# Sparse attention and a PReLU layer on one core: a third value block cast head by head, and the first 600 pieces of a hand-listed order rearranged

## The chip, the cores and the metric

The kernel runs on one core of a Trainium2 chip. A core has a matrix engine (TensorE, "PE" in the profile), whose weight loads are listed apart ("PEld"); a vector engine (VectorE, "DVE"); a scalar engine (ScalarE, "ACT"); a general one (GpSimd, "POOL"); and SyncE ("SP"), which here only issues transfers. Sixteen DMA engines move the data of every queue. Each engine runs its own instructions strictly in its own order, and waits by semaphores for the others. The metric is the device time in microseconds (us) of one execution, and lower is better.

## The reference, cut to what matters

There are 4 batches and 8 heads, each with 768 positions of 64 numbers. Heads 0, 2 and 6 ("retrieval") attend to all earlier positions. The other five ("streaming") attend to the last 64 positions and to the first 4.

```
scores = q @ k^T / 8, masked
a = exp(scores) / sum(exp(scores))
x = a @ v                        # heads side by side: 3072 tokens x 512
h = x @ w_in                     # 512 -> 2048
g = max(h, 0) + alpha * min(h, 0)
out = g @ w_out                  # 2048 -> 512
```

## The kernel before, in words

The heads are taken in pairs, (2,6), (1,5), (0,4) and (3,7), and the work of one batch and one pair is a segment n = 0..15 (n = 4 * batch + pair, L99). Segments 0 to 3 are batch 0. The tokens go through the second layer in eight blocks t: 512 and 256 of each batch (L592).

The program is cut into 1071 named pieces. `ORDER` (L14 to L71) lists their names, written out, and the loop at the end (L826) emits them in just this order. Every engine's queue, and SP's queue of loads, follows from this list: a piece stands on its engine behind all pieces of that engine that are listed earlier. PSUM, where PE writes, has 8 banks. A piece takes banks when it is listed (L145), the one free for longest among those it may use, and has to wait until the piece that gave the bank back has really run. The names are:

- `Lq n`, `Lk n`, `Lv n`: loads of q, k, v of a segment, issued on SP (L204, L216, L231); fp32, 0.393 MB for a pair, a little more for streaming values, whose last 24 rows come as a transfer of their own (L249).
- `Cq n`, `Ck n.head`: their casts to bf16. For segments 0 to 3 nearly all are on POOL (L301, L302). `Cv n`: the cast of both heads' values (L351), on POOL for n < 6. `Cv n.head` casts one head alone (L346): head 0 of the pair on POOL, head 1 on VectorE. A streaming head then has its first four rows copied into six more places (L311).
- `Tq n`, `Tk n`: six transposes on PE each (L360), and `tq n`, `tk n.head`: the copies out of PSUM (L370, L378).
- `S n.head.m`: a part of the scores (L448, L489); `s n.head.m`: its exp, on ACT; `m n.head.m`: a mask on VectorE, from segment 4 on. From segment 4 on, scores that are listed close together are collected (L420): if both heads have at least 576 columns in the collection, the matmuls of the two heads, which use 64 rows of the array each, are interleaved (L433 in the profile), otherwise they are issued one after the other (L426).
- `A n.head`: the product with the values (L559). `a n.head`: division on VectorE (L569, L570). `X n`, `x n`: transposition into `xT` (L584, L589), one part per pair.
- `P t.f`, `p t.f`, `g t.f`: the first layer on PE (L604), the negative part on ACT (L609), the PReLU sum on VectorE (L616). `P0.f.0`, `.1`, `.2` for f < 6 are parts of the first block, which need the pairs 0 and 1, then 2, then 3 (L810). `O t.s.u`, `o t.s`: the second layer (L624) and its way out (L630, L634).
- `wi x`, `wo x`: the weights, issued on POOL (L712, L716), 0.26 MB each as written for `wi`.
- Fills: `kz3` (a zeroed K buffer, POOL), `ro` (the tail of both score buffers of retrieval heads, VectorE, L735), `nz`, `kfz` (POOL), `id` (the identity matrix, POOL), `warm0` to `warm2` (45 matmuls without use at the start, L704).

In `before` only the values of segment 3 are cast head by head:

```
772        if n == 3:
773            for hh in range(2):
774                item(f"Cv{n}.{hh}", cast_v_head, n, hh)
```

Of the kernel before, what the change touches and what calls it, by code (L numbers as in the profile page):

```python
# [23 lines left out]
g1.0 P1.6 P1.4 Lq8 p1.2 one Lq7 g1.2 nz1 wo1 nz0 Tq4 P0.6 wo0 P0.5.0 tk5.1 g0.0 P0.5.1 Lk7 P0.4.0 P0.4.1 p0.6 P0.4.2
g0.6 P0.5.2 p1.6 P0.14 g1.6 Cq6 Tq6 Ck6.0 p1.4 p0.14 g1.4 tq6 P0.13 p0.4 P0.10 g0.14 g0.4 p0.5 kfz0 P1.8 wo2 P0.9 Lv5
p0.13 tq4 g0.5 p1.8 g0.13 g1.8 p0.9 P0.11 Lv4 g0.9 p0.10 S4.0.4 S5.1.2 S4.1.3 Lv6 S4.0.0 p0.11 P1.10 s4.0.0 P0.8 P0.7
g0.10 g0.11 p1.10 S5.0.0 Lk9 g1.10 s5.1.2 p0.8 s4.0.4 g0.8 S4.1.1 S5.0.2 p0.7 S4.1.2 P0.12 s4.1.2 wo3 O0.1.0 s5.0.2
g0.7 s4.1.3 O0.1.1 Ck6.1 p0.12 S5.1.0 g0.12 m4.0.0 s4.1.1 S5.1.1 S4.0.3 m5.1.2 S5.0.1 Lq9 s5.0.0 S4.0.5 S4.1.4 Cv5 Cq7
s4.1.4 Lk8 m4.1.4 m5.0.0 Cq8 s5.0.1 P0.15 O0.3.0 s5.1.1 p0.15 s5.1.0 Tk6 Ck7.0 P1.14 g0.15 S4.1.5 s4.0.3 S4.0.1 s4.0.5
S4.1.0 S4.0.2 O0.3.1 O0.1.2 m5.1.1 m5.1.0 m4.0.4 s4.0.2 p1.14 m5.0.1 s4.1.0 Ck7.1 tk6.1 m4.1.3 m4.1.0 m5.0.2 O0.3.2  # L30
O0.0.0 tk6.0 Tk7 m4.1.1 A5.0 s4.0.1 A5.1 O0.0.1 g1.14 O0.0.2 Cv4 a5.0 Cv6 a5.1 Tq7 O0.3.3 tk7.0 O0.0.3 m4.0.3 O0.1.3
tk7.1 m4.0.5 m4.0.1 s4.1.5 o0.3 tq7 m4.1.5 o0.1 A4.1 S6.0.5 S7.0.0 o0.0 S6.1.2 S6.1.0 S7.0.2 S6.1.1 a4.1 A4.0 s6.1.1
S6.0.4 O0.2.0 s6.1.2 O0.2.1 s6.0.5 Lv7 m6.1.1 s7.0.0 s6.1.0 Cq9 Dq8 Ck8 m6.1.0 S6.0.0 s7.0.2 S7.1.0 s6.0.4 S7.1.2
S6.0.1 S7.1.1 S6.0.3 Dk8.0 m6.0.4 O0.2.2 s6.0.3 s7.1.0 m6.0.3 s7.1.2 X5 Dk8.1 P1.12 s6.0.1 m7.0.2 m6.1.2 Dq9 x5 m6.0.1
s7.1.1 m7.0.0 p1.12 Lv8 Ck9 a4.0 O1.1.0 m6.0.5 g1.12 Cv7 A6.1 ns s6.0.0 O0.2.3 S7.0.1 S6.0.2 m6.0.0 O1.1.1 S8.0.2 nr
O1.1.2 s6.0.2 s7.0.1 Dk9.0 o0.2 A6.0 Lk10 S8.1.0 S8.0.1 m7.0.1 S8.0.3 s8.0.2 S8.1.1 S8.0.0 m7.1.0 a6.1 m7.1.1 S8.1.4
X4 s8.0.1 s8.1.4 a6.0 Dk9.1 Lq10 O1.1.3 s8.1.0 Lv9 A7.0 X6 m7.1.2 a7.0 kfz3 x6 s8.0.0 s8.1.1 A7.1 O1.0.0 O1.0.1 S9.0.0
S8.1.5 s8.0.3 S8.1.2 S9.0.2 o1.1 S8.0.4 a7.1 S8.1.3 X7 s8.1.3 Ck10 m8.1.0 s8.0.4 s8.1.5 O1.0.2 Lk11 s9.0.0 m8.0.3
O1.0.3 x7 P2.4 o1.0 m9.0.0 s8.1.2 S9.1.1 S9.0.1 m8.1.1 m8.1.5 p2.4 S9.1.2 S8.0.5 S9.1.0 m8.0.0 near0 m8.0.1 Lk13
s9.0.2 s8.0.5 s9.1.2 m8.0.4 P2.14 P2.2 s9.1.1 Cv8 s9.0.1 g2.4 m8.1.3 m8.1.4 A8.1 P3.10 P2.3 p2.2 P2.0 g2.2 Cq10 m8.0.5  # L40
a8.1 p2.14 g2.14 p2.0 m9.1.2 P2.1 g2.0 p2.3 P2.7 p2.7 p2.1 A8.0 P3.0 g2.3 P2.5 Ck11 g2.1 P2.9 p2.5 P2.6 g2.7 near2
g2.5 s9.1.0 p3.10 p3.0 p2.9 Cv9 g3.10 P2.8 Lq11 Dk11.1 g2.9 P3.8 m9.1.0 P2.10 p2.8 m9.1.1 Lk12 P3.4 g3.0 A9.1 near1
p2.6 g2.8 Lq13 P2.13 Cq11 P2.15 p2.13 Dk10.1 Dk10.0 Dq10 g2.6 p2.10 g2.13 p3.4 Lq12 P3.6 g2.10 P3.14 p2.15 a9.1 g2.15
P2.11 O2.0.0 P2.12 g3.4 O2.0.1 p2.11 p3.8 g2.11 Ck12 S10.0.1 S10.0.4 s10.0.1 g3.8 p3.14 O2.0.2 s10.0.4 Dk11.0 O2.1.0
Dq11 p2.12 a8.0 g3.14 S10.1.1 S10.0.0 p3.6 g2.12 m10.0.4 S10.1.0 S10.0.5 s10.1.0 s10.1.1 O2.1.1 Lv11 Cq12 O2.0.3 g3.6
S10.0.3 S11.0.0 m10.1.0 s10.0.5 s10.0.0 S11.1.2 S11.1.0 m9.0.2 S10.1.2 S10.0.2 s10.0.3 Cq13 O2.1.2 m10.0.0 s10.1.2
Lv10 Ck13 m9.0.1 m10.1.2 s11.1.2 m11.1.2 s11.1.0 Dk12.0 P3.2 s10.0.2 p3.2 A9.0 s11.0.0 O2.2.0 Dq12 S11.0.2 S11.1.1
m10.0.5 O2.1.3 S11.0.1 m10.0.3 Cv11 m11.0.0 m10.1.1 Dk13.1 m11.1.0 X8 m10.0.1 s11.1.1 Cv10 P3.12 p3.12 m11.1.1 a9.0
s11.0.1 O2.2.1 g3.2 A10.1 Dk13.0 o2.1 Dk12.1 g3.12 a10.1 Dq13 A10.0 A11.1 O2.2.2 m11.0.1 X9 o2.0 O2.3.0 O2.2.3 S12.1.5
S12.0.4 S12.0.2 a10.0 s11.0.2 S12.1.2 m11.0.2 a11.1 S12.0.1 s12.1.5 A11.0 Lq14 a11.0 X11 O2.3.1 O3.1.0 s12.0.4 s12.0.2  # L50
m12.0.4 X10 S13.0.1 O3.1.1 s12.1.2 Lk15 s12.0.1 S12.0.3 S13.0.2 S13.1.2 s13.0.1 S13.1.1 o2.2 S12.0.0 S12.1.0 s12.1.0
s12.0.0 Lk14 s12.0.3 s13.1.2 O2.3.2 Lv12 O2.3.3 m12.0.3 o2.3 O3.0.0 s13.1.1 s13.0.2 O3.1.2 S12.0.5 S13.1.0 S13.0.0
S12.1.4 P4.0 m12.0.1 P4.1 m13.1.2 Cq14 s13.1.0 s13.0.0 m12.1.0 P4.11 m12.0.0 p4.0 s12.0.5 P4.12 m13.1.0 P4.3 p4.1 g4.0
P4.4 m13.0.1 s12.1.4 p4.12 g4.1 Lq15 P5.6 p4.11 m12.0.5 p4.3 g4.11 O3.0.1 m13.1.1 g4.12 Ck15 g4.3 p4.4 P4.15 P4.13
P4.9 p4.13 Lv13 P5.2 p4.15 Ck14 Dq14 m12.0.2 Cv12 g4.4 g4.13 Dk15.1 P4.10 Cq15 g4.15 p5.6 g5.6 p4.10 P4.6 Cv13 Dk14.0
p4.6 g4.10 g4.6 A12.0 p5.2 O3.0.2 A13.1 O3.0.3 g5.2 a13.1 O3.1.3 P4.7 o3.0 S12.1.1 S14.0.3 P4.14 o3.1 P4.2 Dk14.1 p4.7
p4.9 Dq15 s12.1.1 a12.0 g4.7 g4.9 S15.1.2 S14.0.2 p4.14 S14.0.4 S15.1.1 S14.1.0 s14.0.3 m12.1.4 m12.1.1 p4.2 s14.0.2
P5.12 g4.14 m14.0.3 s14.1.0 P4.5 p5.12 g4.2 P4.8 s15.1.2 m13.0.2 O4.3.0 m13.0.0 Lv15 Dk15.0 s14.0.4 p4.5 S14.0.5
S15.1.0 S14.0.1 s15.1.1 S14.1.2 g5.12 g4.5 m15.1.1 p4.8 S12.1.3 g4.8 S14.0.0 s12.1.3 O4.3.1 A13.0 m12.1.3 s14.0.0
# [12 lines left out]


@with_exitstack
def kernel(
    ctx: ExitStack,
    tc: tile.TileContext,
    q: bass.AP,
    k: bass.AP,
    v: bass.AP,  # L80
    is_retrieval: bass.AP,
# [171 lines left out]
    zero = const.tile([128, 1], bf16, name="zero")  # L253
    one = const.tile([128, 1], bf16, name="one")
    ident_f = const.tile([16, 16], fp32, name="ident_f")
    mr = const.tile([128, 5, 144], bf16, name="mr")
    mr_near = const.tile([128, 6, 208], bf16, name="mr_near")
    ms_near = const.tile([128, 3, 176], bf16, name="ms_near")
    ms = const.tile([128, 2, 192], bf16, name="ms")
# [506 lines left out]
    for n in range(NSEG):  # L766
# [2 lines left out]
            item(f"Cq{n}", cast_q, n)  # L769
        item(f"Lk{n}", load_k, n)  # L770
        item(f"Lv{n}", load_v, n)
        if n == 3:
            for hh in range(2):
                item(f"Cv{n}.{hh}", cast_v_head, n, hh)
        else:
            item(f"Cv{n}", cast_v, n)
# [90 lines left out]
```

## Time and profile before

| what | value |
|---|---|
| median of 8 runs | 230.57 us (229.98 to 234.74) |
| the execution that was profiled | 230.94 us, its span 229.2 us |
| PE busy | 220.3 us (96% of the span) |
| DVE, ACT, POOL busy | 153.9, 139.1, 47.1 us |
| TensorE clock granted | full in every slice |

The span runs from the first instruction seen to the last; the other 1.74 us of that execution lie around it. "Busy" is time with at least one instruction of the engine running; PE's instructions overlap each other, so a share of 96% does not say that the array does its most. The chain of waits goes back from the last instruction, at each step to whatever released it. The list of waits names who waited for whom. The timeline lists instructions in order of time, with the idle time ahead of them and its releaser in brackets. All times of day in this text are us from the start of the span.

### The profile page before, as it was taken

Reading aid. Unit: us, or ns where it says so; the run is one execution under the profiler, and the core shown is the slowest. Engines: PE = TensorE matmul, PEld = TensorE weight load, DVE = VectorE, ACT = ScalarE, POOL = GpSimd, SP = SyncE. Lnnn points to the kernel's source line nnn. Section 1 sums busy time; section 2 is a strip of 40 time slices with the busy share of each in tenths; the row PEclk is TensorE's granted clock in tenths of the full one; section 3 lists DMA queues with packets and bytes.
Section 4 is the critical chain, followed back from the end, with each engine's and each line's share of the span. In section 5 each row is a group of like instructions: output and inputs, shape, how many; then the busy total and the mean of one; then the engine's idle time right before and its main releaser. Section 6 shows DMA issues by size and latency. Waiting matters only on the chain.

```text
span 229.2 us, 5203 instructions
## 1 busy us (share of the span) xinstructions
PE 220.3 (96%) x1970; PEld 135.7 (59%) x1998; DVE 153.9 (67%) x395; ACT 139.1 (61%) x280; POOL 47.1 (21%) x96
## 2 busy tenths in 40 slices
PE   6989999999999999999999999999999999999994
PEld 5777866555566656566475445556854555554553
DVE  5688768987857776989997349979990335545110
ACT  5779667999977667654964874498422333623232
POOL 6657876000520733000002100010000020000000
PEclk9999999999999999999999999999999999999999
DMA  6989999999999999799979999893210130110033
GB/s 200 285 207 278 254 243 201 196 235 227 210 226 186 221 235 221 137 219 198 164 148 176 203 234 183 163 232 58 55 36 0 46 140 1 46 46 2 0 137 137
DMA packets 92448, 36.62 MB, mean 160 GB/s; under 512 B 79472, under 2 KB 90632, under 8 KB 92424
## 3 DMA queue, kind: packets, MB, share of 16 engines
q1 hardware_dynamic: 86168, 26.97, 58.4%
q0 software_dynamic: 5792, 8.93, 17.9%
q10 hardware_dynamic: 464, 0.40, 0.5%
q8 instruction: 15, 0.25, 0.5%
q14 instruction: 9, 0.07, 0.1%
HBM read 27.55 MB, written 6.29 MB: 148 GB/s over the span
## 4 chain that ended last, share of the span: by engine, by line
PE 85%; DMA 10%; SPq 1%; issue 1%; DVE 1%; POOL 0%; ACT 0%; DVEq 0%
PE P L604 36%; PE P L624 34%; PE P L559 6%; DMA vf<-in_v_dram 5%; DMA kf<-in_k_dram 5%; PE P L433 4%; PE P L643 2%; PE P L426 1%; PE P L584 1%; PE P L368 1%; SPq L247 1%; SPq L224 0%; SPq L210 0%; DVE vb L348 0%; DVE vb L311 0%
## 5 line engine op out<-in xcount | busy, mean ns | idle before, releaser
L616 DVE SCALAR_TENSOR_TENSOR g<-neg,oma,P 128x512 bf16<-128x512 f32 (+1 forms) x128 | 72.9, 609 | 39.7 <-ACT neg L609 38.6
L604 PE MATMUL P<-xT,w_in_b 128*128 128x256 bf16 (+1 forms) x503 | 89.5, 325 | 0.4
L609 ACT ACTIVATE neg<-P 128x512 f32<-128x512 f32 x96 | 54.3, 608 | 52.2 <-PE P L604 43.4
L624 PE MATMUL P<-w_out_b,g 128*128 128x512 bf16 x349 | 84.3, 379 | 1.5 <-issue 0.6
L604 PEld LDWEIGHTS <-w_in_b 128*128 128x128 bf16 x512 | 48.6, 98 | 32.5 <-DVE g L616 0.4
L624 PEld LDWEIGHTS <-g 128*128 128x128 bf16 x368 | 34.5, 98 | 36.9 <-issue 1.3
L472 ACT ACTIVATE eR<-P 128x448 bf16<-128x448 f32 (+6 forms) x63 | 36.6, 621 | 13.1 <-PE P L433 5.1
L634 POOL DMA_DIRECT2D out_dram<-ot x18 | 9.9, 553 | 117.4 <-ACT ot L630 113.4
L570 DVE TENSOR_TENSOR xn<-P,rcp 128x448 bf16<-128x448 f32 (+1 forms) x32 | 19.4, 608 | 1.1
L630 ACT COPY ot<-P 128x512 f32<-128x512 f32 x23 | 13.2, 594 | 11.0 <-PE P L624 8.6
L526 ACT ACTIVATE eS<-P 128x384 bf16<-128x384 f32 (+1 forms) x25 | 13.5, 570 | 3.6 <-PE P L504 2.6
L520 ACT ACTIVATE eS<-P 128x352 bf16<-128x352 f32 x30 | 13.8, 490 | 1.5 <-PE P L426 1.0
L416 PE MATMUL P<-qT,kT 128*128 128x192 bf16 (+13 forms) x68 | 11.5, 251 | 1.1 <-ACT eR L472 0.6
L559 PE MATMUL P<-vb,eS 128*128 128x65 bf16 x260 | 11.3, 193 | 0.7 <-DVE vb L311 0.4
L559 PEld LDWEIGHTS <-eS 128*128 128x128 bf16 x260 | 10.2, 97 | 2.8 <-issue 1.1
L535 DVE TENSOR_TENSOR eS<-eS,ms_near 128x352 bf16<-128x352 bf16 x30 | 9.3, 332 | 2.3 <-ACT eS L520 2.2
L433 PE MATMUL P<-qT,kT 64*128 64x176 bf16 (+17 forms) x172 | 10.9, 250 | 0.0
L559 PEld LDWEIGHTS <-eR 128*128 128x128 bf16 x276 | 9.6, 97 | 1.5
L569 DVE RECIPROCAL rcp<-P 128x7 f32<-128x7 f32 (+1 forms) x32 | 6.3, 196 | 6.2 <-PE P L559 6.0
L433 PEld LDWEIGHTS <-kT 64*128 64x128 bf16 x172 | 6.8, 94 | 6.0 <-issue 5.7
L559 PE MATMUL P<-vb,eR 128*128 128x65 bf16 x276 | 10.1, 193 | 0.0
L482 DVE TENSOR_TENSOR eR<-eR,mr_near 128x128 bf16<-128x128 bf16 (+5 forms) x36 | 6.8, 222 | 4.3 <-ACT eR L472 4.3
(103 smaller groups left out, 182.4 us busy)
## 6 DMA issues: line engine op xcount, KB each, us to landing
out_dram<-ot POOLq DMA_DIRECT2D x18, 256.0 KB, 3.3
vf<-in_v_dram SPq DMA_DIRECT2D x22, 192.0 KB
kf<-in_k_dram SPq DMA_DIRECT2D x21, 192.0 KB
qf<-in_q_dram SPq DMA_DIRECT2D x18, 192.0 KB
qf<-in_q_dram SPq DMA_DIRECT2D x7, 384.0 KB
w_in_b<-in_moe_w_in_dram POOLq DMA_DIRECT2D x8, 256.0 KB, 9.2
w_out_b<-in_moe_w_out_dram POOLq DMA_DIRECT2D x4, 512.0 KB, 13.7
kf<-in_k_dram SPq DMA_DIRECT2D x9, 196.0 KB
```

The source lines that it names most:

```text
L416: nc.tensor.matmul(to, keys, queries, start=True, stop=stop)
L433: nc.tensor.matmul(to, keys[own], queries[own], start=True, stop=True)
L472: nc.scalar.activation(ebuf[n, hh][:, lo:hi].rearrange("p (x c) -> p x c", x=len(parts)), P[:, got[0]:got[0] + len(parts), 0:(hi - lo) // ...
L520: nc.scalar.activation(slots, sc[:, 0:352].rearrange("p (s c) -> p s c", c=176), AF.Exp, scale=scale)
L526: nc.scalar.activation(slots, sc.rearrange("p x (s c) -> p x s c", c=192), AF.Exp, scale=scale)
L559: nc.tensor.matmul(pav[:, i, :], e[:, o:o + 128], vv[:, j, hh, 0:D + 1], start=(m == 0), stop=(m == len(terms) - 1))
L570: nc.vector.tensor_tensor(xn[n][:, 0:nt, D * hh:D * hh + D], pav[:, :, 0:D], rcp.to_broadcast([128, nt, D]), op=ALU.mult)
L604: nc.tensor.matmul(psg[:, w * i:w * (i + 1)], w_in_b[:, c, 128 * fb:128 * (fb + 1)], xT[:, c, o:o + w], start=(x == 0), stop=(x == 3))
L609: nc.scalar.activation(neg[t, f], bank(held["P", t, f][0]), AF.Relu, scale=-1.0)
L616: nc.vector.scalar_tensor_tensor(g_buf[t % 2][:, fb, 0:w], neg[t, f][:, c], oma[:, fb:fb + 1], bank(got[0])[:, c], op0=ALU.mult, op1=ALU.add)
L624: nc.tensor.matmul(bank(held["O", t, s][0]), g_buf[t % 2][:, f, 128 * s:128 * (s + 1)], w_out_b[:, f, :], start=(f == 0), stop=(f == 15))
L630: nc.scalar.copy(ot, bank(got[0]))
```

## The change

Two things change. The values of segment 2 (heads 0 and 4) are cast head by head too: head 0 on POOL and head 4, with the copies of its first rows, on VectorE.

```diff
-        if n == 3:
+        if n in (2, 3):
             for hh in range(2):
                 item(f"Cv{n}.{hh}", cast_v_head, n, hh)
```

And the list `ORDER` is another one up to its last 71 names; from `m8.1.2 o5.1 g6.5` on both are alike. The list now has 1072 names, as `Cv2` has become `Cv2.0` and `Cv2.1`. What follows is the old list and the new one for the first fifth, and "..." stands for the rest.

```diff
-sz2 kz1 kz3 Lq0.0 zero Lq0.1 id kz0 warm0 Lk0 La kz2 Lk1 nms Cq0.0 nmr qz Tq0.0 Lq1 Ck0.0 qz0 warm1 Tk0.0 Lq2 Lk2 mr
-warm2 vz3 Ck0.1 Cq0.1 Ck1.1 tk0.0 m14.0.2 tq0.0 Lv0 Ck1.0 S0.0.1 Tk0.1 vz1 sz1 tk0.1 s0.0.1 Lk3 S0.0.0 Cq1 Tq0.1 Lv1
-Cq2 vz0 Ck2.1 S0.0.2 Ck2.0 vz2 s0.0.0 tq0.1 Cv0 Ck3.0 Tk1 Lq3 Tq1 sz0 s0.0.2 Lq5 so tq1 S0.1.2 vo s0.1.2 S0.1.0 s0.1.0
-Lv2 Tq2 S0.1.1 Ck3.1 tk1.0 tk1.1 S1.0.1 Tk2 s0.1.1 tk2.1 tk2.0 s1.0.1 S1.0.0 A0.0 Cv1 tq2 A0.1 a0.0 wi0 a0.1 s1.0.0
-S2.1.1 S2.1.0 s2.1.1 Tk3 S2.0.0 Cq3 s2.1.0 m4.0.2 m10.0.2 X0 wi1 s2.0.0 Cv2 S2.0.1 S1.1.1 Cq5 x0 s2.0.1 Tq3 tk3.0 ro
-Lk4 s1.1.1 Ck4.1 S1.1.0 tk3.1 tq3 wi2 s1.1.0 A1.0 S2.0.2 A2.1 S3.1.1 a1.0 Lv3 Ck4.0 Cv3.0 a2.1 Lk5 A1.1 s2.0.2 idf
-s3.1.1 S3.1.0 A2.0 s3.1.0 S3.0.0 a1.1 X1 a2.0 S3.0.1 x1 s3.0.1 kfz1 s3.0.0 Tk4 Cv3.1 wi3 wi6 X2 m6.0.2 Tq5 x2 A3.1
-P0.2.0 Lq6 tk4.0 a3.1 A3.0 P0.3.0 Ck5.0 Lq4 tk4.1 a3.0 wi7 P0.0.0 wi5 ms P0.1.0 Al kfz2 X3 Ck5.1 P0.1.1 Tk5 tq5 wi4
-tk5.0 x3 P0.0.1 P0.2.1 P0.3.1 P0.1.2 P0.0.2 P0.3.2 Cq4 P1.2 al p0.1 g0.1 p0.3 Lk6 P0.2.2 P1.0 p0.2 g0.3 p1.0 g0.2 p0.0
+kz1 sz1 zero La Lq0.0 qz id warm0 Lk0 kz0 qz0 nms sz2 vz2 Cq0.0 nmr vz0 kz2 sz0 Ck0.1 vz1 Tq0.0 Ck0.0 so warm1 Lk1
+Lq0.1 Ck1.0 Tk0.0 Cq0.1 tq0.0 tk0.0 vz3 Ck1.1 warm2 Lq1 Cq1 Lk2 S0.0.0 S0.0.1 Tk0.1 Lq2 one Cq2 nz0 Tq0.1 tk0.1 Tq1
+s0.0.0 s0.0.1 S0.0.2 Tk1 idf kfz0 tq0.1 Ck2.1 s0.0.2 S0.1.2 S0.1.0 Lv0 tq1 Lk3 Ck2.0 tk1.0 s0.1.2 s0.1.0 S0.1.1 Cv0
+Ck3.1 ro Ck3.0 Lv1 m10.0.2 Tq2 tk1.1 Tk2 vo S1.1.1 s0.1.1 kz3 Cv1 wi0 Lv2 s1.1.1 tq2 mr A0.0 kfz2 wi1 Lq3 A0.1 Lk4
+tk2.1 S1.0.1 tk2.0 Cq3 Cv2.0 Lq5 S1.0.0 a0.1 a0.0 s1.0.1 wi3 S2.0.0 s1.0.0 Tk3 s2.0.0 Cq5 S1.1.0 A1.0 S2.1.0 nz1
+s1.1.0 S2.0.2 s2.1.0 Tq3 s2.0.2 Lv3 S2.1.1 X0 S2.0.1 tk3.0 a1.0 Cv2.1 x0 s2.1.1 tq3 A2.1 tk3.1 A1.1 a1.1 kfz1 S3.0.1
+Tq5 a2.1 Ck4.0 s2.0.1 S3.0.0 kfz3 Ck4.1 A2.0 Lk5 wi2 s3.0.1 S3.1.0 s3.0.0 wi6 X1 a2.0 Cv3.0 Tk4 wi7 x1 Ck5.0 X2 x2
+S3.1.1 s3.1.0 Cv3.1 A3.0 s3.1.1 P0.1.0 Ck5.1 a3.0 P0.0.0 P0.1.1 A3.1 wi5 P0.2.0 P0.3.0 P0.2.1 Lq6 tq5 P0.0.1 a3.1 nr
+X3 P0.3.1 Lq4 x3 wi4 tk4.0 Tk5 P1.0 Al al Lk6 P0.1.2 tk4.1 P0.2.2 tk5.0 tk5.1 P0.3.2 p0.2 p0.1 g0.2 Lk7 P0.6 P1.6 p0.6
...
```

PE issues as many instructions in both. The collected scores of segments 4 to 15 fall into 26 collections before, 16 of them interleaved, and into 28 after, 17 of them interleaved.

## The prediction

> **What bounds the kernel now.** I read the windows first, then the chain of waits, then PE's own waits, then POOL's and VectorE's timelines in the first 30 us. The windows, with the columns length, PE, PEld, DVE, ACT, POOL:
>
> ```profile
> 0.00:28.60 28.60, 24.38 (x369) 21.39 (x370) 21.31 (x56) 20.69 (x27) 20.09 (x43) 1.00 0.99 245
> 28.60:50.00 21.40, 21.24 (x170) 13.07 (x173) 17.78 (x41) 17.75 (x36) 7.79 (x13) 1.00 1.20 219
> 50.00:100.00 50.00, 49.37 (x486) 29.44 (x493) 37.78 (x108) 37.79 (x85) 12.67 (x29) 1.00 1.07 210
> ```
>
> PE idles 4.22 us up to 28.6 and then 0.16 us in 21.4 and 0.63 in 50. After 28.6 its list of waits has one or two pieces of 0.16 us a stretch, put down to "issue", and nobody's data. So 28.6 us is where a start limited by loads ends and pure matrix work begins: an order can win in the start, 2.2 us of it before the first matmul (PE waits 2.21 us for the identity matrix), and afterwards only lose, or do less matrix work. The chain at that point:
>
> ```profile
> 15.03 4.92 DMA vf<-in_v_dram
> 19.96 7.36 DMA vf<-in_v_dram
> 27.41 0.57 DVE vb L348
> 28.00 0.55 DVE vb L311
> 28.60 0.51 PE P L559 x11
> ```
>
> The last values of batch 0 (segment 3) land at 27.32, VectorE casts head 1, and PE resumes A3.1 at 28.60 after idling 0.35. A3.1 is there the first product of segment 3. All other work of batch 0 up to there is done: I call it D.
>
> **The change, part by part.**
>
> *The split cast.* POOL loses one 128x896 cast of 0.93 and one copy of 0.34 and gets a 128x448 cast of 0.56: -0.71. VectorE gets 0.56 + 0.54 from its rows of segment 3: +1.10. The values of segment 2 move ahead of q3, k4 and q5 on SP, so they land about 3 us earlier, and VectorE's idle time, 1.4 us between 22 and 28, covers it. Worth by itself: nothing, since A2.1 waited just 0.18 us for POOL. Without that cover it costs 1.10.
>
> A rule speaks against this half. In the row, a 128x448 cast on VectorE takes 557 ns beside POOL's work, where a 128x384 one (L333) takes 352 later on. The Trainium skill, SBUF — State Buffer, section "SBUF: two separate sides", says that VectorE and GpSimd hold a shared port pair exclusively, each blocking the other for a whole instruction. By that rule the split could cost POOL up to the 0.56 it saves; by the row it costs VectorE some 0.2 us. No row of POOL is seen to lengthen.
>
> *The last values.* Ahead of segment 3's values SP has issued the same bytes in both orders (5.34 MB including them), so they still land near 27.3. But the third of the weight transfers, wi3 now, is issued behind Cv2.0, near 20.9; before, wi2 was the third, issued at 23.93, and none of its bytes moved before 28. SP's queue moved 0.39 MB from 22 to 26 with the weights' queue active (0.43 MB), and 0.54 MB from 26 to 28 with it quiet. If wi3 fills that quiet time, the last 0.33 MB go at 0.1 per us for 2.3 us (0.26 MB at 0.11), then at 0.27: landing at 28.7. Bounds 27.3 and 28.7; I take 28.2. With 1.1 us for cast and copy A3.1 can start at 29.3. The new order puts A3.0 (0.39) and five parts of P0 (1.08) first, so PE reaches it about 1.47 us after A3.0's start: hidden, if A3.0 starts after 28.
>
> *The start.* The memset kz3 (0.84) no longer stands ahead of the identity on POOL: the first matmul comes 0.78 us earlier. The first transpose waits for Cq0.0, whose q lands at 4.09, and comes at 4.65, not 5.31. This 0.66 is lost at Tq1: Cq1 waited for q1 until 8.51 and ended at 9.34, with as many bytes ahead of it now. I take 0.
>
> *ro.* This is the dearest step. In before it ran late, behind no idle time:
>
> ```profile
> 12.07 0.92 DVE L395 COPY kT<-P 64x744 bf16<-64x744 bf16 x1
> ...
> 20.69 0.33 DVE L293 MEMSET eR<- 128x328 f32 x1
> ```
>
> Now it stands between tk1.0 and tk1.1, and by the built program's waits it waits for the exp s0.1.0. ACT ran the three exps of that head from 11.81 to 14.35; with tq1 and the exps in the new sequence, s0.1.0 ends near 14.0 (the three earlier exps up to 11.5, tq1 0.79, two exps of 0.88). Then ro 0.33, tk1.1 1.14 (0.85 + 0.09 + 0.20): 15.5. Tk2 needs the bank that tk1.1 gives back: 15.55, where before it began at 14.39. Queued behind ro on VectorE are tk1.1, vo, mr and tk2; behind Tk2 on PE all the rest. Behind s0.1.1, which waits for ro in turn, stands s1.1.1.
>
> From Tk2 to A3 PE has 12.56 us of work by its rows (24 pieces: 0.34 a transpose group, 0.33 to 0.66 a score part, 0.39, 0.64 or 0.82 a value product), plus 0.35 for a part of S1 that came earlier before. Without idle time A3.0 is reached at 15.55 + 12.9 = 28.46; I add 0.2 for exps that PE outruns. In before, this stage took 13.63, so its idle time was 1.07; that is the upper end, 29.5. If ro costs nothing, Tk2 waits only for its cast (14.25) and A3.0 comes at 27.2, the lower end.
>
> *POOL ahead of Cv3.0.* In before:
>
> ```profile
> 22.71 0.82 POOL L320 CAST natq<-qf 128x768 bf16<-128x768 f32 x1
> 23.48 0.50 POOL L333 CAST natm<-kf 128x384 bf16<-128x384 f32 x1
> ...
> 25.44 0.56 POOL L348 CAST vb<-vf 128x448 bf16<-128x448 f32 x1 [0.40 <-DMA vf<-in_v_dram]
> ```
>
> Cv3.0 was limited by its load, and done with its copy at 26.4. Now POOL does Cq5, two memsets (0.84, 0.15), Ck4 twice with a memset (1.05), two weight issues (1.22) and then Cv3.0: from Cq5's start 0.77 + 3.26 + 0.97 = 5.0 us. Cq5 waits for q5, now behind k4: it lands between 21.4 (v2 in before) and 24.5 (k4's second cast in before), say 23.5. So Cv3.0 is ready at 26.4 to 29.5, say 28.5: beside the PE's 28.46, hardly later.
>
> *Sum of the start.* A3.0 at 28.7 after D. Before, A3.1 stood at 28.60 with 2 of its 13 matmuls done, worth 28.55. From there both have the same matrix work: **+0.15**, bounds -1.35 (27.2) and +0.95 (29.5).
>
> *Matrix work afterwards.* Collected scores: the columns that PE walks, the longer half where heads are interleaved and the sum elsewhere, are 25464 before and 24888 after. 576 columns at 2.37 per ns (512 in 0.216 us): **-0.24**.
>
> *Later stalls.* After 28.6 before has 1.9 us of idle time, most of it "issue". Summed by the rows' durations along both lists, ACT and VectorE have the same work against PE's progress to within 3.3 us at every point; VectorE's comes up to 2.9 us earlier between PE's 44th and 70th us of work. VectorE was 76% busy from 50 to 100, so it fits. Bounds 0 and 2; I take **+0.3**, near "nothing", because the row of before is nothing.
>
> *Sum:* +0.15 - 0.24 + 0.3 = +0.2. Against the profiled 230.94: 231.15. That execution was 0.37 above the median of 230.57, so on the scale of the runs **230.8**.
>
> **Rivals.**
>
> *Faster: the start is really shorter.* For it: POOL's and PE's idle time in the first 28 us, 2.0 us of PE's after its first matmul, and values ready earlier. Against it: ro's wait and the bytes ahead of q1, q5 and v3. If ro's wait is hidden, A3.0 starts at 27.2: -1.35 - 0.24 = -1.6: 229.0.
>
> *Slower: banks run out when the first layer starts.* ACT now copies both heads of k5 (tk5.0, tk5.1) before its first piece of the first layer, p0.2; in before it did one (32.45 to 33.32) and then started p0.1. Tk5 comes near 32.9, so p0.2 starts near 34.7, 1.4 us later, and every PReLU sum gives its bank back 1.4 later. By my count PE has filled the last bank near 37.3 and the first sum ends near 36.0, so there are 1.3 us in hand; if PE gets there 1.3 sooner in relation, or if VectorE's sums (0.74) fall behind PE's 0.87 a piece, PE stalls from 36 us on, up to the whole 1.4. Then +0.15 - 0.24 + 0.3 + 1.4 = +1.6: 232.2. For it: VectorE waited 1.41 us for its first sum already; against it: PE has no wait for a sum after 28.6 that is worth naming.
>
> *The split does not matter and the rest cancels.* v2 was not on the chain, v3 lands when its bytes have passed. Then only the columns count: 230.3.
>
> **How the numbers follow.** About 0.5% (1.15 us) is what a measurement of this kernel can tell from no change. The forecast (230.8, its own range 229.7 to 231.7 by the bounds of the start) gets 0.50; the cancelling case 0.05; both are "same". The bank stall gets 0.25, and 0.08 goes to stalls of the unseen later order that reach their bound of 2 us (232.5 to 233): "slower" 0.33. The faster rival gets 0.12. The range 229.3 to 232.9 leaves out about 0.1 on each side.
>
> **What would show it.** VectorE's memset of eR near 14 us, and PE idle for over a us ahead of Tk2: ro's step. PE's first L559 of segment 3 near 28.7, released by POOL's vb or by nothing. L604 released by VectorE's L616 or PE idle near 36 to 40: the bank rival. Segment 3's last values landing after 28: wi3's step. PE idle time from 30 us on above 3 us would make the forecast wrong, as would A3.0 before 27.5.

## The result and the profile after

The changed kernel takes **233.52 us** (median of 11 executions, 232.13 to 235.54) where the kernel before takes 230.72 (32 executions beside it): 1.0132 of it, with a 95% interval of 1.0106 to 1.0159. That is 2.8 us slower, and outside the range that was forecast. The execution that was profiled took 232.75 us (span 231.1), 0.8 below that median, so the profile shows only part of the loss. Keep that in mind; much of what follows is about the other part.

The windows of after, with the columns length, PE, PEld, DVE, ACT, POOL, granted clock, DMA share and GB/s:

```profile
0.00:28.60 28.60, 23.53 (x359) 20.66 (x360) 21.03 (x56) 19.91 (x25) 21.27 (x46) 1.00 0.98 241
28.60:50.00 21.40, 21.17 (x179) 13.71 (x179) 16.99 (x36) 17.73 (x36) 7.15 (x10) 1.00 1.20 230
50.00:100.00 50.00, 49.41 (x477) 28.65 (x484) 36.67 (x109) 37.49 (x84) 12.46 (x27) 1.00 1.04 201
```

PE idles 5.07 us up to 28.6, before 4.22; behind that there is nothing to tell the two apart. PE's whole list of waits in after, with the columns total us, times, longest:

```profile
PE P L368 <- DVE kT L397: 1.5, 1, 1.5
PE P L707 <- POOL ident masks.py:199: 1.4, 1, 1.4
PE P L416 <- ACT eR L472: 1.2, 2, 0.7
PE P L368 <- POOL g L320: 0.9, 1, 0.9
PE P L559 <- ACT kT L391: 0.2, 1, 0.2
```

The identity matrix comes 0.8 us earlier than before (1.4 against 2.2), and four waits between 9 and 16 us take back more than that. The largest is ro's. Three rows of the timeline of after, first VectorE's, then PE's for Tk2 and A3.0:

```profile
14.21 0.33 DVE L293 MEMSET eR<- 128x328 f32 x1 [1.54 <-ACT eR L472]
15.76 0.50 PE L368 MATMUL P<-ident,g 128*128 128x128 bf16 x6 [1.51 <-DVE kT L397]
29.01 0.55 PE L559 MATMUL P<-vb,eS 128*128 128x65 bf16 x13
```

VectorE stands 1.54 us for the exp, ro runs at 14.21, and PE stands 1.51 us ahead of Tk2. A3.0 comes at 29.01. The last copy on ACT ends at 227.75 us, before at 226.67: **+1.1 us** is what this execution lost on its way.

Another **0.7 us** of its longer span lies behind that copy, in the tail: 3.3 us to the end against 2.6. SyncE waits there for the last output transfer. One line of SyncE's list of waits, of before and then of after (total us, times, longest):

```profile
SPq L862 <- DMA out_dram<-ot: 1.6, 3, 0.7
```

```profile
SPq L862 <- DMA out_dram<-ot: 2.3, 3, 1.5
```

The tail goes with the split. Over the twenty profiles of this study it is 2.5 to 2.6 us in all nine in which VectorE casts no values of segment 2 (before, e5, e7, e10, e11, e12, e14, e15, e17), and 3.0 to 3.5 us in all eleven in which it does (after, e1 to e4, e6, e8, e9, e13, e16, e18).

### The profile page after: what moved, and what is told of

The parts are those of the page before. It is cut to its first block, busy times and chain, and to the rows that moved or that the text cites. A ratio compares the mean times of both kernels' runs of the same rounds, so it can differ in the third digit from the quotient of the medians.

```text
span 231.1 us, 5201 instructions
## 1 busy us (share of the span) xinstructions
PE 220.8 (96%) x1972; PEld 135.0 (58%) x1998; DVE 154.4 (67%) x397; ACT 140.5 (61%) x280; POOL 47.8 (21%) x95
## 4 chain that ended last, share of the span: by engine, by line
PE 81%; DMA 7%; SPq 4%; POOL 2%; ACT 2%; issue 1%
PE P L604 35%; PE P L624 33%; PE P L559 5%; DMA kf<-in_k_dram 5%; PE P L433 4%; DMA qf<-in_q_dram 3%; PE P L643 2%; SPq L224 1%; SPq L249 1%; PE P L426 1%; POOL g L333 1%; PE P L584 1%; ACT eR L472 1%; PE P L368 1%; SPq L293 0%
## 5 line engine op out<-in xcount | busy, mean ns | idle before, releaser
L616 DVE SCALAR_TENSOR_TENSOR g<-neg,oma,P 128x512 bf16<-128x512 f32 (+1 forms) x128 | 72.3, 609 | 37.0 <-ACT neg L609 33.2
L604 PE MATMUL P<-xT,w_in_b 128*128 128x256 bf16 (+1 forms) x500 | 88.7, 325 | 0.6
L624 PE MATMUL P<-w_out_b,g 128*128 128x512 bf16 x354 | 85.4, 380 | 0.7
L609 ACT ACTIVATE neg<-P 128x512 f32<-128x512 f32 x96 | 55.2, 607 | 47.0 <-PE P L604 40.6
L604 PEld LDWEIGHTS <-w_in_b 128*128 128x128 bf16 x512 | 48.8, 98 | 32.6 <-issue 0.5
L634 POOL DMA_DIRECT2D out_dram<-ot x18 | 10.5, 585 | 122.7 <-ACT ot L630 122.6
L570 DVE TENSOR_TENSOR xn<-P,rcp 128x448 bf16<-128x448 f32 (+1 forms) x32 | 19.4, 608 | 1.1
L416 PE MATMUL P<-qT,kT 128*128 128x192 bf16 (+12 forms) x68 | 11.1, 251 | 1.2 <-ACT eR L472 1.2
L559 PEld LDWEIGHTS <-eS 128*128 128x128 bf16 x260 | 9.6, 97 | 2.5 <-issue 0.5
L433 PE MATMUL P<-qT,kT 64*128 64x176 bf16 (+14 forms) x174 | 10.9, 250 | 0.0
L559 PE MATMUL P<-vb,eS 128*128 128x65 bf16 x260 | 10.5, 193 | 0.2 <-ACT kT L391 0.2
L589 DVE COPY xT<-P 128x768 bf16<-128x768 bf16 x8 | 4.5, 557 | 8.2 <-PE P L584 7.4
```

The costliest lines, as they stand in the source:

```text
L416: nc.tensor.matmul(to, keys, queries, start=True, stop=stop)
L433: nc.tensor.matmul(to, keys[own], queries[own], start=True, stop=True)
L559: nc.tensor.matmul(pav[:, i, :], e[:, o:o + 128], vv[:, j, hh, 0:D + 1], start=(m == 0), stop=(m == len(terms) - 1))
L570: nc.vector.tensor_tensor(xn[n][:, 0:nt, D * hh:D * hh + D], pav[:, :, 0:D], rcp.to_broadcast([128, nt, D]), op=ALU.mult)
L604: nc.tensor.matmul(psg[:, w * i:w * (i + 1)], w_in_b[:, c, 128 * fb:128 * (fb + 1)], xT[:, c, o:o + w], start=(x == 0), stop=(x == 3))
L609: nc.scalar.activation(neg[t, f], bank(held["P", t, f][0]), AF.Relu, scale=-1.0)
```

## The experiments

Each ran beside the kernel before on the same chip; its median there was 230.8 to 231.2 us. Each profile shows one execution. The theories at the start: the loss is ro alone; or k5's late landing at the first layer (in after GpSimd waits 2.17 us for it, until 32.45); or a stall later on; or the half clock of TensorE.

**e1: Tk5 behind the first pieces of the first layer.**

```diff
-tk4.0 Tk5 P1.0
+tk4.0 P1.0
...
-P0.2.2 tk5.0 tk5.1 P0.3.2
+P0.2.2 P0.3.2
...
-P0.6 P1.6 p0.6
-g0.1 P0.5.0
+P0.6 P1.6 Tk5 p0.6
+g0.1 tk5.0 tk5.1 P0.5.0
```

> The changed kernel with the transposes of k5 (Tk5) listed two pieces of the first layer later, behind P1.6, and the two copies tk5.0, tk5.1 behind g0.1. Theory K (the median's excess of 2.8 us comes mostly from PE standing at Tk5 for the second head of k5, which lands at 32.39 in the profile of the changed kernel and later in other executions): Tk5 gets 2.6 us more of work ahead of it, the median falls by 1.5 to 2.2 us to 231.3 to 232.0 and the spread of the runs narrows. Theory R (the start alone, by the memset ro): no change, 233.5. Theory L (stalls after 40 us): no change.

Measured: 236.36 us, 1.0205 (1.0169 to 1.0240). Worse, so k5 is not what the first layer lacks; moving its copies behind makes PE wait for VectorE's sums (L368 and L604 on L616, 1.1 us together). A part of the loss in its profile is something else, told with e9.

**e2: ro late.**

```diff
-Ck3.1 ro Ck3.0
+Ck3.1 Ck3.0
...
-S2.0.1 tk3.0 a1.0
+S2.0.1 tk3.0 ro a1.0
```

> The changed kernel with the memset ro moved back behind tk3.0, its place before. Theory R: VectorE does not wait for the exp, Tk2 starts near 14.1 instead of 15.76, PE reaches A3.0 at 27.7 to 28.2 instead of 29.01, and the time falls by 0.8 to 1.3 us. Theory K: PE only reaches Tk5 earlier and waits there longer, the time falls by 0 to 0.2. Theory L: the time falls by 0.8 to 1.3 and stays above before.

Measured: 231.81 us, 1.0043 (1.0014 to 1.0072). By the ratios (0.0132 - 0.0043 of 231 us) this one step gives back 2.1 of 3.0 us. Yet A3.0 comes at 27.12, 1.9 earlier than in after, and the kernel is still not faster than before. PE's first product of the first layer in this run:

```profile
28.47 1.24 PE L604 MATMUL P<-xT,w_in_b 128*128 128x512 bf16 x4 [0.80 <-DMA w_in_b<-in_moe_w_in_dram]
```

It stands 0.80 us for the weights. PE cannot use the early A3.0.

**e3: the third weight transfer late.**

```diff
-a0.1 a0.0 s1.0.1 wi3
+a0.1 a0.0 s1.0.1
...
-wi2 s3.0.1
+wi2 wi3 s3.0.1
```

> The changed kernel with the third weight transfer wi3 issued behind wi2, near 26 instead of 21.3. Theory K with the weights' queue as the cause of k5's late landing: k5's second head lands 1 to 2 us earlier (30.4 to 31.4), PE does not wait at Tk5, the median falls by 1 to 2 us. If k5 is late for another reason: no change, or slower by up to 1 us if P0.6 then waits for wi3. Theories R and L: no change.

Measured: 234.15 us, 1.0123 (1.0084 to 1.0162). k5 now lands early (its casts start at 28.90 and 29.55, in after at 29.78 and 32.45), and nothing is gained: k5's late landing is not the loss. A wait appears that after's profile lacks: PE for VectorE's `eR` near 77 us, 1.0.

**e4: the split cast alone, in the kernel before.**

```diff
-wi1 s2.0.0 Cv2 S2.0.1
+wi1 s2.0.0 Cv2.0 S2.0.1
...
-S2.0.2 A2.1
+S2.0.2 Cv2.1 A2.1
...
-        if n == 3:
+        if n in (2, 3):
```

> The kernel before with nothing but the split of the cast: Cv2.0 in Cv2's place on POOL, Cv2.1 on VectorE ahead of A2.1. All theories: within 0.3 us of before (230.7), as the values of segment 2 were not on the chain. If the split itself costs (VectorE's copies 1.1 us later in the start), 231.2 to 231.8.

Measured: 232.25 us, 1.0051 (1.0022 to 1.0080): +1.2 us for a step that the prediction put at nothing. In its profile A2.1 waits for VectorE twice, 0.29 and 0.19. The last copy on ACT ends at 227.23, 0.56 later than before, and the tail is 0.4 longer: 1.0 in all.

**e5: the split undone in the changed kernel; e6: the changed kernel once more.**

```diff
-Cv2.0
+Cv2
...
-Cv2.1 A2.1
+A2.1
...
-        if n in (2, 3):
+        if n == 3:
```

> The changed kernel with the values of the third pair cast whole on GpSimd again (Cv2 in the place of Cv2.0, Cv2.1 dropped), all else as in the changed order. Theory 'ro alone' (the memset ro placed early is the whole loss): within 0.4 us of the changed kernel's 233.5. Theory 'split costs too' (the split alone in the old order measured 232.25 against 230.83): 0.8 to 1.4 us faster than the changed kernel, 232.1 to 232.7, and the wait of A2.1 for VectorE's cast is gone.

> The changed kernel unchanged, a second profiled execution beside this set's runs of the kernel before. Its first profiled execution lies 0.8 us under its own median. Theory 'half clock': the long executions (span over 232.5) have a mean granted clock of at most 0.995, since 3.6 us at 0.50 take 0.008 off the mean. Theory 'more idle time': long executions keep 0.997 or more, and TensorE idles longer at 8 to 16 us than the 3.7 us the first profile shows there, or loses it behind 28 us, where the first profile shows nothing.

Measured: e5 232.26 us, 1.0058 (1.0028 to 1.0089); e6 234.14, 1.0116 (1.0084 to 1.0148). So the split too makes up more than half of the loss, 1.7 us by the ratios of after and e5, and "ro alone" falls. But after's profile has no wait for a cast of values at all. e6 also shows what e3 showed. VectorE's cast of pair 9's queries and PE's product behind it, in e6:

```profile
76.95 0.56 DVE L320 CAST natq<-qf 128x768 bf16<-128x768 f32 x1 [2.29 <-DMA qf<-in_q_dram]
```

```profile
77.70 0.97 PE L559 MATMUL P<-vb,eR 128*128 128x65 bf16 x25 [1.08 <-DVE eR L482]
```

The load `Lq9` is now issued behind the transposes Dk8 on SP; VectorE waits 2.29 us for it (1.00 in after), and the masks queued behind that cast are late for PE.

**e7 and e8: hybrids.** The old order up to A3.1 and then the changed one; and the changed one up to A3.0 and then the old one.

> Hybrid: the old order up to A3.1 (everything that the start holds, ro late, the whole cast Cv2), then the remaining pieces in the changed order. Theory 'the loss is in the start': like before or better by the 0.24 us of fewer columns, 230.4 to 231.0. Theory 'the loss is also behind the start' (the changed order of the first layer and of the scores costs idle time that the one profiled execution did not show): 231.5 to 232.5.

> The other hybrid: the changed order up to A3.0 (ro early, the cast split), then the remaining pieces in the old order. Theory 'the loss is in the start': 233 to 234, as the changed kernel. Theory 'the loss is behind the start': 231.0 to 231.5, with only the 0.5 us by which A3.0 came later in the profile.

Measured: e7 233.88 us, 1.0094 (1.0057 to 1.0131); e8 233.33, 1.0100 (1.0072 to 1.0127). As a test of where the loss lies they fail, since both lose: at the seam of e7 the fills kfz0 to kfz3, which the changed order has early, come all at once on GpSimd. But that accident shows a mechanism. VectorE's cast of the last values in e7, then GpSimd at that time, then A3.1 on PE:

```profile
27.72 1.85 DVE L348 CAST vb<-vf 128x448 bf16<-128x448 f32 x1
```

```profile
27.09 0.93 POOL L293 MEMSET natk<- 128x960 f32 x1
27.92 0.38 POOL L293 MEMSET kf<- 128x128 f32 x2
28.22 0.93 POOL L293 MEMSET natk<- 128x960 f32 x1
29.06 0.24 POOL L293 MEMSET kf<- 128x128 f32 x1
```

```profile
29.63 0.22 PE L559 MATMUL P<-vb,eS 128*128 128x65 bf16 x2 [1.14 <-DVE vb L348]
```

A cast that takes 0.42 us elsewhere takes 1.85 here: it comes to an end only when GpSimd's row of memsets does, and PE waits 1.14 us for it.

**e9: q9's load ahead of the transposes; e10: that, ro late, and the split undone.**

```diff
-m4.0.5 Dk8.1
+m4.0.5 Lq9 Dk8.1
...
-Dk8.0 m6.1.1 Lq9 Ck9
+Dk8.0 m6.1.1 Ck9
```

> The changed kernel with one load moved: the queries of pair 9 (Lq9) issued ahead of the transposes Dk8.1 and Dk8.0 on SyncE's queue instead of behind them. Theory 'late q9' (VectorE's cast Cq9 near 76 us waits 1.0 to 2.3 us for that load in all profiles that hold the changed order's later part, and TensorE loses up to 1.1 us behind it in some): the load is issued near 66 instead of 69.5 us, the wait at Cq9 is gone, and the median falls by 0.3 to 0.8 us against the changed kernel, to 1.009 to 1.011 of before. Theory 'start alone': no change, 1.012 to 1.013 of before.

> The changed order with all three suspects undone: ro behind tk3.0, the third pair's values cast whole on GpSimd, q9's load ahead of the transposes. If these three make up the loss, what remains is the earlier identity matrix and the 576 fewer columns: 230.3 to 231.0, 0.997 to 1.001 of before. If something else of the new order costs too (the first weights, which the run with ro late waited for by 0.8 us): 1.002 to 1.005.

Measured: e9 236.26 us, 1.0168 (1.0117 to 1.0219); e10 232.01, 1.0038 (1.0015 to 1.0061). The wait only changed its name. One line of PE's list of waits in e10, which e2 and after do not have:

```profile
PE P L433 <- DMA kT<-natk: 0.8, 1, 0.8
```

Now the transposed keys are late. e9 has a second trouble, as e1 had. The windows of e9 around Tk2, where the granted clock is the third number from the end:

```profile
14.00:15.00 1.00, 0.00 (x0) 0.00 (x0) 0.97 (x3) 0.81 (x1) 0.23 (x2) 1.00 0.23 44
15.00:16.00 1.00, 0.69 (x9) 0.67 (x9) 0.88 (x6) 0.11 (x1) 1.00 (x2) 0.84 0.88 203
16.00:17.00 1.00, 1.00 (x19) 1.00 (x18) 1.00 (x3) 0.52 (x2) 1.00 (x3) 0.50 1.04 206
17.00:18.00 1.00, 1.00 (x22) 1.00 (x20) 0.96 (x2) 0.66 (x1) 0.94 (x3) 0.50 0.63 122
18.00:19.00 1.00, 1.00 (x18) 0.98 (x16) 0.20 (x1) 0.00 (x0) 1.00 (x3) 0.50 0.99 356
19.00:20.00 1.00, 1.00 (x14) 0.93 (x13) 0.94 (x3) 0.49 (x1) 1.00 (x3) 0.96 1.04 375
```

Right behind the idle time ahead of Tk2 TensorE runs at half its clock for some 3.4 us (by these windows), and A0's 42 matmuls take 2.48 us where they take 1.43 in after.

**e11: ro early, alone, in the kernel before.**

```diff
-tk1.0 tk1.1 S1.0.1
+tk1.0 ro tk1.1 S1.0.1
...
-tk3.0 ro
+tk3.0
```

> The kernel before with only the memset ro moved to where the change has it, between the two halves of the copy tk1 on VectorE. Direct price by the prediction's working: ro waits for the last exp of the second head (14.35) and pushes Tk2 from 14.39 to about 15.9, so TensorE idles 1.5 us ahead of Tk2; with 1.07 us of idle time in the stage behind it to swallow some, 0.5 to 1.5 us of the time: 1.002 to 1.006 of before. Theory 'half clock' adds executions with a mean granted clock of 0.991 to 0.993, which before has none of.

Measured: 231.42 us, 1.0006 (0.9981 to 1.0031). Tk2 comes at 15.64 after 1.13 us of idle time, as the working of the prediction would have it, but A3.1 starts at 28.53 and without a wait, where before had it at 28.02 with a wait inside, until 28.60. The idle time of that stage swallows ro, and the time is the same within what can be measured.

**e12: as e10, and the first two weight transfers issued earlier.**

```diff
-kz3 Cv1 wi0 Lv2
+wi0 kz3 Cv1 wi1 Lv2
...
-kfz2 wi1 Lq3
+kfz2 Lq3
```

> As the run that undoes all three, and the first two transfers of the first layer's weights issued earlier on GpSimd: wi0 ahead of the memset kz3, wi1 right behind Cv1. If the weights hold the first layer's first product (0.8 us in the run with ro late), TensorE's wait for them is gone and the median lies 0.3 to 0.8 us under that run, 0.995 to 0.999 of before. If they take bandwidth from the keys and queries of batch 0 in return, the same or slower.

Measured: 233.49 us, 1.0088 (1.0060 to 1.0117). Slower. In its profile, of an execution 3.5 us above that median, GpSimd waits 2.7 us for q3 and PE 2.5 us behind it (L368 on `g`): the earlier weights seem to take bandwidth from the start's own loads.

**e13 to e16**, four questions at once: the cast of q9 moved instead of its load; the split kept, but both halves on GpSimd; a version with what had looked best; and ro's delay lengthened.

```diff
-s6.0.3 Cq9 s8.0.1 Dq9 m6.0.1
+s6.0.3 s8.0.1 m6.0.1
...
-s8.0.2 m7.1.2 A6.0
+s8.0.2 m7.1.2 Cq9 Dq9 A6.0
```

> The changed kernel with the cast Cq9 (and the transfer Dq9 that follows it) moved behind the masks m6.0.1 to m7.1.2 on VectorE, so that a late q9 holds up no mask that TensorE needs. Theory 'late q9': TensorE's wait for VectorE's eR near 77 us (0 to 1.1 us) cannot occur, the median lies 0.3 to 0.8 us under the changed kernel's, 1.009 to 1.011 of before. Theory 'start alone': 1.012 to 1.013. If the later cast makes the scores of pair 9 wait, a wait of L433 for the transposed q appears in its place and the time does not fall.

```diff
-        cast_of("PV"[hh])(vv[:, :, hh, 0:D], vf[n % NF][:, :, hh, :])
+        cast_of(("PP" if n == 2 else "PV")[hh])(vv[:, :, hh, 0:D], vf[n % NF][:, :, hh, :])
```

> The changed kernel with the third pair's values still cast head by head at the same two places, but both on GpSimd. Theory 'VectorE as the place' (its queue is blocked by the values' landing and is 0.66 to 1.1 us longer in the start): like the kernel with the whole cast on GpSimd, 1.005 to 1.007 of before. Theory 'two pieces in this order': no gain, 1.011 to 1.013.

e15 joins the edits of e2, e5 and e13.

> The changed order with ro behind tk3.0, the whole cast of the third pair on GpSimd, and Cq9 with Dq9 behind the masks (the load Lq9 where the change has it). If the three are the loss and their cures add up: 230.3 to 231.0, 0.996 to 1.000 of before. If the start keeps another loss (waits for GpSimd's casts of q1 and for the first weights): 1.003 to 1.005, as the run that undid three with the load moved.

```diff
-Ck3.1 ro Ck3.0
+Ck3.1 ro ro2 ro3 Ck3.0
...
+    fill("ro2", eR_all[:, :, FAR.RTOT:E_R].bitcast(fp32), ONES)
+    fill("ro3", eR_all[:, :, FAR.RTOT:E_R].bitcast(fp32), ONES)
```

> The changed kernel with the memset ro written three times in a row (the same value), so that tk1.1 and Tk2 come 0.66 us later and TensorE idles 2.2 us ahead of Tk2 instead of 1.5. Theory 'half clock after a long idle': most executions have a mean granted clock of 0.993 or less (3.6 us at 0.50), and the median rises by 2 to 3 us, to 1.02 to 1.025 of before. Theory 'only the delay': the clock stays at 0.997 and above and the median rises by 0.5 to 0.7 us, to 1.014 to 1.016.

Measured: e13 234.37 us, 1.0113 (1.0060 to 1.0166); e14 233.89, 1.0126 (1.0073 to 1.0179); e15 231.10, 1.0017 (0.9990 to 1.0044); e16 234.87, 1.0172 (1.0128 to 1.0215).

e13 cannot be told from the changed kernel. Its profile is the most telling one of the study, because up to 74 us it is the changed kernel, in another execution than the one shown above. VectorE in e13:

```profile
22.16 1.69 DVE L348 CAST vb<-vf 128x448 bf16<-128x448 f32 x1
...
30.08 1.76 DVE L348 CAST vb<-vf 128x448 bf16<-128x448 f32 x1
```

GpSimd in e13 at those two times:

```profile
21.73 0.85 POOL L320 CAST natq<-qf 128x768 bf16<-128x768 f32 x1
22.50 0.92 POOL L293 MEMSET natk<- 128x960 f32 x1
23.33 0.23 POOL L293 MEMSET kf<- 128x128 f32 x1
...
30.27 1.28 POOL L679 TENSOR_SCALAR_AFFINE_SELECT mr_near<-one 128x1248 bf16<-128x1248 bf16 x1
```

PE in e13:

```profile
31.89 0.83 PE L559 MATMUL P<-vb,eS 128*128 128x65 bf16 x13 [0.51 <-DVE vb L348]
```

And the same two casts in after, where GpSimd stood waiting for loads at both times:

```profile
21.79 0.41 DVE L348 CAST vb<-vf 128x448 bf16<-128x448 f32 x1
22.24 0.25 DVE L311 COPY vb<-vb 4x192 f32<-4x192 f32 x1
...
29.34 0.42 DVE L348 CAST vb<-vf 128x448 bf16<-128x448 f32 x1
```

```profile
22.67 0.83 POOL L320 CAST natq<-qf 128x768 bf16<-128x768 f32 x1 [0.73 <-DMA qf<-in_q_dram]
23.43 0.90 POOL L293 MEMSET natk<- 128x960 f32 x1
...
29.78 0.50 POOL L333 CAST natm<-kf 128x384 bf16<-128x384 f32 x1 [1.58 <-DMA kf<-in_k_dram]
```

If q5 and k5 land a little earlier, or VectorE comes a little later, GpSimd's memset and select meet VectorE's casts, and each cast takes 1.3 us longer. Up to 74 us it is one program with two courses.

e14 says that leaving VectorE does not help in this place: GpSimd reaches Cv2.1 only at 23.79, and A2.1 waits for it. PE in e14:

```profile
24.41 0.22 PE L559 MATMUL P<-vb,eS 128*128 128x65 bf16 x2 [0.61 <-POOL vb L348]
24.81 0.37 PE L559 MATMUL P<-vb,eS 128*128 128x65 bf16 x7 [0.18 <-POOL vb L311]
```

e16 tests the clock: PE idles 2.44 us ahead of Tk2, and its profile runs at full clock all the same. By the ratios it costs 0.9 us beyond after (0.0040), and its idle time there is 0.93 longer. That fits a price of the idle time's own length; a half clock does not follow from it each time (two of its six executions have a mean clock of 0.993 or less).

**e17: ro late and the split undone, nothing else; e18: both in the kernel before.** Their edits are those of e2 with e5, and of e11 with e4.

> The changed order with ro behind tk3.0 and the third pair's values cast whole on GpSimd; the load and the cast of q9 as the change has them. Theory 'ro and the split are the loss': as the run with the cast of q9 moved too, 1.000 to 1.003 of before. Theory 'q9 has a share of its own': 1.003 to 1.006, and where its profile shows VectorE's wait at Cq9 above 1.5 us, TensorE waits behind it near 77 us.

> The kernel before with both steps and no other: ro between the two halves of tk1, and the third pair's values split (first head on GpSimd in the place of Cv2, second on VectorE ahead of A2.1). Alone they measured 1.0006 and 1.0051. Theory 'the two make the loss anywhere': 1.010 or more. Theory 'they add up': 1.005 to 1.007. Theory 'they cost what the new start makes of them, where the three exps wait for the second copies of q and k': at most 1.005.

Measured: e17 231.11 us, 0.9993 (0.9960 to 1.0026); e18 232.40, 1.0067 (1.0036 to 1.0098). **With ro and the split undone nothing that could be measured is left of the loss**, q9 has no share of its own that could be seen, and the rest of the new order is worth nothing that could be seen either way. In the old order the two add up (0.0006 + 0.0051 against 0.0067). In the new order, counted from e17, the split alone (e2) costs 0.0050, ro alone (e5) 0.0065, and both (after) 0.0139: 1.2, 1.5 and 3.2 us. The sum of the two, 2.7, is within the intervals of the 3.2. No version beats the kernel before. In e18's profile, as in e4's, the last copy is late (0.4 us) and the tail is 0.4 longer.

## Why the prediction was wrong, point by point

**The split cast is the step that failed first.** "Worth by itself: nothing", with VectorE's 1.4 us of idle time as cover, was wrong: it costs 1.2 us in the old order (e4) and 1.2 to 1.7 in the new (e2 against e17, after against e5). The cover is there in after's profile (0.92 us of idle time behind the cast and its copy, which took 0.66 and not 1.10). Two costs stood at nothing in the sum. One is the tail, longer in every profile with this cast on VectorE: by 0.4 us in e4 and e18, 0.5 in e2, 0.7 in after and e6. With the 0.56 by which its last copy is late, that is 1.0 of e4's 1.2. The other is the length of the casts when they meet GpSimd's work. These are all the profiled executions that hold the changed start, ro and split included; the casts are those of segments 2 and 3 on VectorE:

| execution | cast 2, us | cast 3, us | A3.1 at | last copy ends |
|---|---|---|---|---|
| after | 0.41 | 0.42 | 30.48 | 227.75 |
| e6 (the same kernel) | 0.50 | 0.43 | 29.95 | 228.27 |
| e3 | 0.41 | 0.43 | 30.39 | 228.80 |
| e8 (old order later) | 0.41, its copy 1.74 | 0.66 | 30.90 | 228.91 |
| e13 | 1.69 | 1.76 | 31.89 | 229.19 |
| e16 (ro thrice) | 1.48 | 1.69 | 31.68 | 229.39 |
| e9 (with half clock) | 1.21 | 1.82 | 32.33 | 231.18 |
| e1 (with half clock) | 0.76 | 1.28 | 31.75 | 231.27 |

In the lower half both casts meet GpSimd's work. What that costs PE can be read at full clock from Tk2 to the transposition of alpha (`Al`, L658), the same pieces in all of these: 18.3 to 18.7 us in after, e3 and e6, 19.6 in e13 and 19.4 in e16, so 0.7 to 1.3 us for the two collisions. Both profiled executions of the changed kernel had missed them, and they lie 0.8 and 0.9 us under the medians of their sets (233.52 and 234.14). That its unprofiled executions split in two courses, and that this makes up those 0.8 us, is inferred from these eight, not seen. Single executions differ as much for other reasons: e17 was profiled at 233.15 us, 2.0 above its own median, without a collision, and its last copy ends at 228.88, later than after's. With ro late or the split undone, the last values' cast runs at 27.5 to 29.6 us, ahead of the select; it took 0.42 in e2, e5, e10, e15 and e17, and 1.12 only in e12, whose start had been held up by 2.5 us. So the price of ro alone (e5) and of the split alone (e2) in the new order does not rest on a collision, as far as their profiles show.

**The rule was there and was weighed the wrong way round.** In e7 and e13 the rows show VectorE casts that end only behind GpSimd's memsets or select. The Trainium skill, SBUF — State Buffer, section "SBUF: two separate sides", says of the pair of ports that the two share: for VectorE instructions of a two-port mode it is an exclusive lock, held for a whole instruction, not a split of bandwidth. No row tells the mode of the cast. The prediction asked what the lock would cost POOL, looked for a long row of POOL, found none, and priced VectorE's side at 0.2 us from one row that had met a DMA issue and a short cast. The runs fit the rule and give a price on VectorE: 0.42 becomes 1.2 to 1.85 (0.76 in one). In e7 the cast outlasts a row of four GpSimd memsets, not one instruction. Which of the two began first cannot be read (in e13 the cast's row starts 0.19 us ahead of the select's and ends 0.29 behind it).

**ro: the working held, its price did not.** Forecast were ro at 14.0, Tk2 at 15.55, A3.0 at 28.7; they came at 14.21, 15.76 and 29.01. The direct loss of the start was +0.46 instead of +0.15. The same memset costs 0.1 us in the old order (e11), where A3.1 waits for the last values anyway, and 1.5 to 2.1 in the new (e5 against e17, after against e2). The forecast took the start for something that pays both ways. It does not. PE in six profiles with the same pieces from A3.0 to Al:

| execution | ro | A3.0 at | Al at | last copy ends |
|---|---|---|---|---|
| e2 | late | 27.12 | 33.14 | 226.66 |
| e15 | late | 28.02 | 33.08 | 226.51 |
| e17 | late | 27.74 | 34.85 | 228.88 |
| e6 | early | 28.49 | 33.55 | 228.27 |
| after | early | 29.01 | 34.32 | 227.75 |
| e5 | early | 29.24 | 34.30 | 228.03 |

With nothing in between, Al comes 5.06 us behind A3.0 (e5, e6, e15), and the last copy 193.4 to 194.0 behind Al, longer only in e6, which waits 1.08 for q9. Between e15 and e5, whose orders differ up to Al only in ro's place, A3.0 moves by 1.2 us, Al by 1.2, and the last copy by 1.5. An A3.0 before 28.0 gains nothing (e2, e17).

**The faster rival was wrong at its root.** It gave 229.0 for an A3.0 at 27.2. In e2 A3.0 came at 27.12 and in e17 at 27.74, and neither is faster than before. What PE meets next is late for other reasons, by the profile: in e2 the weights (0.80, shown above), in e17 a copy on ACT and then k5, for which GpSimd's cast waited 2.19 us:

```profile
29.16 1.24 PE L604 MATMUL P<-xT,w_in_b 128*128 128x512 bf16 x5 [0.87 <-ACT qT L373]
...
33.53 0.51 PE L368 MATMUL P<-ident,natm 128*128 128x128 bf16 x6 [0.84 <-POOL natm L333]
```

So what PE gains ahead of 28 us it loses by 34, and what it loses there stays lost. The lower bound of -1.35 stood on a gain that no run shows.

**What held.** The gain of 0.77 us at the first matmul is lost at Tq1, which waits 0.85 us for q1 (the 0.9 in PE's list). The last values are no limit by their load. Without a collision A3.1 follows A3.0 by 1.47 us (29.01, 30.48), as worked out. The bank rival did not happen: PE has no wait for a PReLU sum in after; e1 shows that such a wait can be made, and that it costs. The 0.24 us for fewer columns cannot be read: PE's busy time is 220.8 and 221.9 us in two executions of the same program. The later stalls, put at 0.3 with bounds of 0 and 2, were by PE's named waits behind 28.6 us 0.2 in after and 1.25 in e6; the late q9 behind the latter was not among the rivals, and by e17's median it has no share that could be seen.

**What stays open.** How many unprofiled executions of the changed kernel have the collision. And why two instructions more on VectorE (397 in after, 395 before) come with a longer tail: that was not tested. In after, e1, e2, e3, e6, e9, e13 and e16 a transfer of 8 KB on a queue that the profile calls "instruction" starts 1.0 to 1.4 us behind the last copy, and the last output packet ends 1.6 to 1.9 behind it. In the other twelve that transfer starts 1.7 us behind the copy or later, and the last output packet ends at 1.2. But in e4, e8 and e18, which are among the twelve, the tail is 0.4 longer all the same.

## What to carry to other kernels

Price a piece that is moved to VectorE by its slowest neighbour on GpSimd, not by its own row: ask which GpSimd memset, select or cast can run at that time if the loads come a microsecond earlier or later. A median that lies well above its own profile can mean that the profile caught a good course; take several before explaining the difference. Compare the time behind the last copy too, over all profiles: here it told the kernels with the split from those without. And an earlier arrival in this start was worth only what the next load allowed, while a later one was paid in full.

## What the runs showed of the hardware

TensorE fell to half its clock for about 3.4 us right behind an idle gap of 1.51 us (e9, e1) and one of 2.54 us (e12), while 1.51 us in after and 2.44 us in e16 left it at full clock. The Trainium skill, TensorE: Matmul & The Clock Gate, Part 1, names an idle window of about 3.4 us and a window that runs freely; the half rate and a dependence on chance agree, a gap of 1.51 us is less than half of the time that it names. Other idle time of PE lies close ahead of it in e9 (0.67 us at 11.14, 0.51 at 12.87); whether it counts was not tested. By the mean granted clock (0.993 or less) it struck 18 of the 72 executions of kernels with the new start and ro early, 2 of the changed kernel's 18 among them, and 1 of 55 with the new start and ro late. But it struck 4 of 10 of e7, which has the old start with ro late, 3 of the 107 of the kernel before that ran beside the experiments, and none of 24 of e11 and e18, which idle 1.13 us ahead of Tk2. So the gap ahead of Tk2 is not its only cause; it adds to the loss in some executions, and is not what makes the median.

A load queued behind transposing transfers came late here: with Lq9 behind Dk8, VectorE's cast of q9 waited 0.4 to 2.3 us for it in all ten profiles that have load and cast where the change has them, and with Lq9 ahead of them the transposed keys came 0.8 to 1.5 us late for PE instead.
